# One kernel, five edits: weight words joined in PSUM, shorter scale steps, queries scaled at landing, stores issued by ScalarE, and a list schedule fed with other durations

## The chip, the cores and the metric

The kernel runs on one core of a Trainium2 chip as one program. The time is that of the device for the whole program, in microseconds (us), as the median of a few runs. One execution was also recorded by the hardware profiler; every duration, wait and clock below is from that execution. Engines are named as the profile names them: PE (matmuls), PEld (its weight loads), DVE (VectorE), ACT (ScalarE), POOL (GpSimd) and SP, whose queue issues transfers. A "q" behind a name (SPq, POOLq) is the engine's own instruction queue.

## The reference

Three parts, one behind the other, over 4 batches of 576 tokens with 8 heads of 64. All sums are wanted in float32 accuracy, which the kernel gets by splitting each operand in a high and a low part and multiplying hi·hi, hi·lo and lo·hi.

```
# attention, per batch and head: keep only scores within tau of the row's maximum
scores = (q @ k.T) / 8
scores = where(scores >= max(scores) - tau, scores, -1e9)
x = softmax(scores) @ v                          # 2304 x 512 after all heads

# dense block; w_in 512x2048 and w_out 2048x512 are float64
h = x @ w_in
x = (h * tanh(softplus(h))) @ w_out

# routed block: 8 experts, one per token, and a token with x @ w_skip <= 0 passes through
e = argmax(x @ w_gate); g = softmax(x @ w_gate)[e]
out = x + g * (relu(x @ w1[e]) @ w2[e])
```

## The kernel before

**Units.** Attention runs in 144 units, a unit being 128 query rows against all 576 keys of one head (of two heads for the last, half-filled query tile of a batch). A unit goes score (PE, into the PSUM tile `s`, of which there are two), `u_max` (DVE, row maximum, negated, `nm`), `u_thr` (DVE, two small instructions: the mask's limit and the exponent's bias), `u_exp` (ACT), `u_mask` (DVE, compares with the limit and multiplies), `u_hi` and `u_lo` (a float16 high and low part `hl`), `u_tr` (a transposing DMA on SP's queue, `hl` to `pt`), `u_pv` (PE, times the values). The first 16 units do their mask on PE instead. Queries land raw; the factor 1/8 is applied inside `u_exp`.

**Weights.** `w_in` and `w_out` come as 64-bit floats, 16 chunks each. `w_conv` makes 32-bit words of a chunk with three DVE instructions in SBUF and one addition on POOL (`w_add`); `w_square` then multiplies the words on PE into `gram`, a reduction over partitions on POOL (`all_reduce`) and `w_scale` (`pow2_scale`: seven tiny DVE instructions in a row) give a power of two, and `w_hi`, `w_lo` split the scaled words. The same kind of reduction and scale is taken for each batch of values (`v_scale`), for the gate's weights and for the experts' first weights.

**Dense and routed blocks.** The dense block works on blocks of 128 or 256 tokens as they come out of attention (`m_g1`, `m_exp` to `m_lo`, `m_g2`, `m_out`, `m_store`). `m_store` puts two transfers of a finished tile on SP's queue. Experts follow when attention and the dense block are through.

**What sets the order.** Class `Plan` is a list scheduler that runs while the program is built. Each step is an `op` with an engine (or two engines with a duration each, of which the planner picks one), a duration in ns, a priority, what it comes after, and which ring of buffers it takes and frees. `solve` walks a clock forward and gives each free engine the ready step of best priority; `emit` writes the program in the order found. On the chip every engine runs its steps strictly in that order and waits where a step's input is not there. The reductions over partitions stand in the plan with 400 ns.

Of the kernel before, what the change touches and what calls it, by code (L numbers as in the profile page):

```python
# [20 lines left out]

def pow2_scale(nc, pool, total, s, inv, top=205):
# [168 lines left out]
class Route:  # L191
# [33 lines left out]
    def weights(s):  # L225
        nc = s.nc
        sq = s.wg16[:, 0]
        nc.scalar.activation(out=sq, in_=s.wg, func=AF.Square, accum_out=s.wsc[:, 0:1])
# [16 lines left out]
    def rsq(s, ts, xs):  # L245
        s.begin(ts, xs)
        d = s.st[ts]
        h = d["h"] = s.wk.tile([128, 2, 2, DM], F16, tag="u", bufs=s.nu, name="rh")
        for i, x in enumerate(xs):
            s.nc.scalar.activation(out=h[:, i, 0], in_=x, func=AF.Square, accum_out=d["ss"][:, i])  # L250
# [20 lines left out]
    def psq(s, ts):  # L271
        d = s.st[ts]
        h = d["h"] = s.wk.tile([128, 2, 2, DM], F16, tag="u", bufs=s.nu, name="rh")
        s.nc.scalar.activation(out=h[:, 0, 0], in_=d["x"][0], func=AF.Square, accum_out=d["ss"][:, 0])
# [6 lines left out]
    def rinv(s, ts):  # L281

        d = s.st[ts]
        pow2_scale(s.nc, None, d["ss"], d["inv"], d["rin"], 195)
# [109 lines left out]
class Second:  # L394
# [27 lines left out]
    def stat(s, e, k):  # L422
        t = s.raw.pop(("s", e, k))
        s.nc.scalar.activation(out=t, in_=t, func=AF.Square, accum_out=s.sq[:, e, k:k + 1])  # L424
# [307 lines left out]
def body(ctx, tc, q, k, v, tau, w_in, w_out, w_skip, w_gate, w1, w2, out):  # L732
# [110 lines left out]
    def w_conv(which, c):  # L843

        t = stage[which, c]
        d = wst(c).bitcast(I32)
        lo, hi = t[:, :, 0], t[:, :, 1]
        nc.vector.tensor_scalar(out=d, in0=hi, scalar1=3, scalar2=0x3FFFFFFF, op0=ALU.logical_shift_left,
                                op1=ALU.bitwise_and)
        m = conv_mode(which, c)  # L850
        if m != "D":
            nc.vector.tensor_scalar(out=lo, in0=lo, scalar1=29, scalar2=None, op0=ALU.logical_shift_right)
        if m == "P":
            nc.vector.tensor_scalar(out=hi, in0=hi, scalar1=-(1 << 30), scalar2=None, op0=ALU.bitwise_and)
        else:
            nc.vector.scalar_tensor_tensor(out=d, in0=hi, scalar=-(1 << 30), in1=d, op0=ALU.bitwise_and,
                                           op1=ALU.bitwise_or)
        if m == "D":
            nc.vector.scalar_tensor_tensor(out=d, in0=lo, scalar=29, in1=d, op0=ALU.logical_shift_right,
                                           op1=ALU.bitwise_or)  # L860

    def w_add(which, c):
        t = stage[which, c]
        d = wst(c).bitcast(I32)
        nc.gpsimd.tensor_tensor(out=d, in0=d, in1=t[:, :, 0], op=ALU.add)
        if conv_mode(which, c) == "P":
            nc.gpsimd.tensor_tensor(out=d, in0=d, in1=t[:, :, 1], op=ALU.add)
# [10 lines left out]
    def w_total(which):  # L878
        nc.vector.scalar_tensor_tensor(out=junk32, in0=gram.pop(which)[:, 0:128], scalar=1.0, in1=ident, op0=ALU.mult,
# [59 lines left out]
    def v_square(b, j):  # L939
# [3 lines left out]
        nc.scalar.activation(out=junk, in_=t, func=AF.Square, accum_out=sqv[:, b, j:j + 1])  # L943
# [18 lines left out]
    def q_load(b, qt, c):  # L962
# [7 lines left out]
        stage["q", b, qt, c] = t  # L970

# [39 lines left out]
    def u_max(i):  # L1011
        nm = att.tile([128, 1], F32, tag="nm", bufs=4, name="nm")
# [3 lines left out]
    def u_thr(i):  # L1016

        th = att.tile([128, 2], F32, tag="th", bufs=4, name="th")
        nm, lim = nmx.pop(i), lambda: nc.vector.tensor_scalar(out=th[:, 1:2], in0=nm, scalar1=-1.0, scalar2=ntau[:, 0:1],
                                                              op0=ALU.mult, op1=ALU.add)  # L1020
        if on_pe(i):
            lim()
        nc.vector.tensor_scalar(out=th[:, 0:1], in0=nm, scalar1=0.125, scalar2=None, op0=ALU.mult)  # L1023
        if not on_pe(i):
            lim()
        thr[i] = th
# [684 lines left out]
```

## Time and profile before

| | |
|---|---|
| median of 3 runs | 1104.58 us (1104.17 to 1106.23) |
| profiled execution | 1109.86 us, of which its instructions span 1107.9 us |
| PE / DVE / ACT / POOL busy | 832.0 / 823.4 / 603.7 / 536.2 us |
| mean granted clock of PE | 0.879 of full speed |

The median of the runs is 5.3 us under the profiled execution. The page gives busy time for each engine; "idle before" of a group of instructions is the time its engine stood still just before them, with what released it.

### The profile page before, as it was taken

What the parts mean: (1) busy time and instruction counts of PE and PEld (TensorE: products, weight loads), DVE (VectorE), ACT (ScalarE), POOL (GpSimd) and SP (SyncE); (2) the same over time, 40 slices, a digit from 0 to 9 for tenths busy, and PEclk for the clock granted to TensorE, in tenths of its full rate; (3) what the DMA queues carried; (4) which work ended last, traced back from release to release, by engine and by line L of the source; (5) the groups of instructions that cost most, each with busy time, mean ns of one, the idle gap of its engine ahead of it and who ended that gap; (6) DMA issues with size and microseconds to landing.
All of it is one profiled execution on the core that took longest, in us unless ns stands there. A gap on an engine that the chain in (4) does not pass through costs nothing. (4 is left out here: it accounts for less than half of the span.)

```text
span 1107.9 us, 20418 instructions
## 1 busy us (share of the span) xinstructions
PE 832.0 (75%) x7412; PEld 623.0 (56%) x7412; DVE 823.4 (74%) x1744; ACT 603.7 (54%) x951; POOL 536.2 (48%) x455
## 2 busy tenths in 40 slices
PE   5684375688267888887698989688859988687865
PEld 3353364566155666664476666566626647576764
DVE  5898298898467888878788999898637668474552
ACT  4337144667474676686477677666645743232330
POOL 2561766575435544444645564363325425453443
PEclk9996685689698998899899999889979988888898
DMA  9763295557274495694465674576533418776650
GB/s 260 252 178 93 82 206 138 130 116 195 46 162 93 84 210 116 158 190 81 112 151 133 158 172 108 115 153 140 130 101 109 134 39 264 216 216 197 223 190 26
DMA packets 254148, 162.76 MB, mean 147 GB/s; under 512 B 205135, under 2 KB 205519, under 8 KB 254032
## 3 DMA queue, kind: packets, MB, share of 16 engines
q1 hardware_dynamic: 251136, 154.45, 55.6%
q0 software_dynamic: 2896, 6.83, 2.0%
q8 instruction: 65, 1.06, 0.4%
q14 instruction: 51, 0.42, 0.1%
HBM read 100.71 MB, written 12.57 MB: 102 GB/s over the span
## 5 line engine op out<-in xcount | busy, mean ns | idle before, releaser
L1170 PE MATMUL hp<-xt,win 128*128 128x256 f16 (+1 forms) x1920 | 222.4, 275 | 2.2 <-ACT g L802 2.2
L1227 PE MATMUL o<-wout,g 128*128 128x512 f16 x816 | 199.5, 398 | 18.9 <-POOL g L1216 15.3
L1170 PEld LDWEIGHTS <-win 128*128 128x128 f16 x1920 | 177.3, 103 | 29.4 <-issue 2.8
L1009 PE MATMUL s<-kt,qh 128*128 128x288 f32 x320 | 116.9, 379 | 85.4 <-DVE e L1063 53.6
L1227 PEld LDWEIGHTS <-g 128*128 128x128 f16 x816 | 80.3, 102 | 110.9 <-issue 19.0
L1013 DVE TENSOR_REDUCE nm<-s 128x1 f32<-128x576 f32 x144 | 105.8, 749 | 37.3 <-PE s L1009 36.8
L1096 PE MATMUL xps<-vt,pt 128*128 128x64 f16 (+1 forms) x2016 | 98.0, 209 | 44.0 <-DMA pt<-hl 38.2
L1075 POOL TENSOR_TENSOR hl<-e,hl 128x512 f16<-128x512 f32 x107 | 130.2, 1217 | 0.0
L1074 POOL TENSOR_TENSOR hl<-e,hl 128x64 f16<-128x64 f32 x107 | 47.9, 448 | 166.5 <-ACT hl L802 74.3
L1009 PEld LDWEIGHTS s<-kt,qh 128*128 128x128 f32 x320 | 70.1, 219 | 103.5 <-issue 68.1
L1048 ACT ACTIVATE e<-s,th 128x576 f32<-128x576 f32 x128 | 90.8, 735 | 68.2 <-DVE th L1023 45.3
L1063 DVE SCALAR_TENSOR_TENSOR e<-s,th,e 128x576 f32<-128x576 f32 x128 | 101.4, 810 | 23.4 <-ACT e L1048 23.2
L1096 PEld LDWEIGHTS <-pt 128*128 128x128 f16 x2016 | 85.1, 107 | 58.6 <-DMA pt<-hl 44.9
L1009 PE MATMUL s<-kt,ql 128*128 128x288 f32 x320 | 101.2, 329 | 0.3 <-DVE ql L981 0.3
L802 ACT ACTIVATE hl<-e 128x576 f16<-128x576 f32 x94 | 63.0, 679 | 44.1 <-DVE e L1063 27.8
L576 PEld LDWEIGHTS <-w1q 128*128 128x128 f16 x1056 | 68.9, 107 | 22.3 <-POOL w1q L488 7.2
L1206 POOL TENSOR_TENSOR u<-u,g 128x1024 f32<-128x1024 f32 x22 | 53.7, 2446 | 50.5 <-ACT u L1202 43.2
L599 PE MATMUL o<-w2q,ht 128*128 128x512 f32 x264 | 65.8, 404 | 12.3 <-POOL w2q L488 4.0
L1009 PEld LDWEIGHTS s<-kt,ql 128*128 128x128 f32 x320 | 71.2, 223 | 1.2 <-DVE ql L981 0.7
L576 PE MATMUL g<-xt,w1q 128*128 128x128 f16 x864 | 59.1, 235 | 16.1 <-POOL w1q L488 6.9
L1216 POOL TENSOR_TENSOR g<-u,g 128x1024 f16<-128x1024 f32 x22 | 51.1, 2326 | 29.0 <-ACT g L802 17.2
L424 ACT ACTIVATE ws<-ws 128x512 f32<-128x512 f32 x64 | 40.0, 625 | 44.8 <-DMA ws<-in_w_dram 43.9
(237 smaller groups left out, 1677.8 us busy)
## 6 DMA issues: line engine op xcount, KB each, us to landing
stage<-in_w_dram SPq DMA_DIRECT2D x32, 1024.0 KB, 7.0
ws<-in_w_dram SPq DMA_DIRECT2D x64, 256.0 KB, 3.2
qst<-in_q_dram SPq DMA_DIRECT2D x38, 256.0 KB, 3.9
vst<-in_v_dram SPq DMA_DIRECT2D x35, 256.0 KB, 4.3
win<-in_moe_w_in_dram SPq DMA_DIRECT2D x16, 512.0 KB, 5.9
w<-in_moe_w_out_dram SPq DMA_DIRECT2D x16, 512.0 KB, 4.6
kst<-in_k_dram SPq DMA_DIRECT2D x24, 288.0 KB, 3.1
x2d<-ob SPq DMA_DIRECT2D x18, 256.0 KB, 2.5
```

Source lines behind the costliest of these rows:

```text
L576: s.nc.tensor.matmul(out=p[:, f], lhsT=w[:, c, a, k, f * 128:(f + 1) * 128], rhs=xt[:, 4 * b + k], start=m == 0, stop=m == 11)
L599: s.nc.tensor.matmul(out=o, lhsT=ht[:, a, k], rhs=w[b][:, k // 4, k % 4, :], start=m == 0, stop=m == 23)
L802: nc.scalar.activation(out=out, in_=in_, func=AF.Copy, scale=scale)
L1009: nc.tensor.matmul(out=o, lhsT=x, rhs=y, start=start and n == 0, stop=n == len(ops) - 1)
L1013: nc.vector.tensor_reduce(out=nm, in_=sp[i][:, :, 0:HS], axis=AX.XY, op=ALU.max, negate=True)
L1048: nc.scalar.activation(out=e, in_=sp[i][:, :, 0:HS], func=AF.Exp, scale=0.125, bias=thr[i][:, 0:1])
L1063: nc.vector.scalar_tensor_tensor(out=ep[i], in0=sp.pop(i)[:, :, 0:HS], scalar=thr.pop(i)[:, 1:2], in1=ep[i], op0=ALU.is_ge, op1=ALU.mult, ...
L1075: ENG[eng].tensor_tensor(out=t[:, S + 64:2 * S], in0=e[:, 0:512], in1=t[:, 0:512], op=ALU.subtract)
L1096: nc.tensor.matmul(out=o, lhsT=p[:, blk, :], rhs=vv[:, a, h0:h0 + w], start=(n == 0), stop=(n == len(seq) - 1))
L1170: nc.tensor.matmul(out=hp[j, p][:, i * TB:(i + 1) * TB], lhsT=win[wa][:, kk, f * 128:(f + 1) * 128], rhs=xt[j][:, xa, kk, 0:TB], start=(n ...
L1206: ENG[eng].tensor_tensor(out=u, in0=u, in1=gt[j, r], op=ALU.mult)
L1227: nc.tensor.matmul(out=o, lhsT=g[:, ga, i * TB + s * 128:i * TB + (s + 1) * 128], rhs=wout[f // 8][:, f % 8, wa, :], start=(f == 0 and n = ...
```

## The change

Five edits in one. (1) `w_conv` writes its two intermediate steps to a PSUM tile `wbits` (from the ring `h`, two buffers, that also takes the dense block's `hp`), and its third DVE instruction brings in the low word; POOL's 32 additions are gone. (2) `pow2_scale` has four instructions in place of seven: the sums it gets are taken doubled, by a factor of the square root of two inside the squaring; the routing's `rinv` now calls it once for each tile of a pair. (3) `q_scale`, new, multiplies each landed query tile by 1/8 in place (38 times on ACT, one of the two first tiles on ACT and one on DVE); `u_exp` takes the negated maximum itself as its bias, so `u_thr` is one instruction and `u_exp` comes after `u_max` alone. (4) `m_store` issues its two transfers from ACT. In the same vein `x_evac` adds its 1e-9 on ACT. (5) Most durations given to the planner are others; with them the planner moves steps between engines and changes their order.

```diff
 def pow2_scale(nc, pool, total, s, inv, top=205):
-    nc.vector.tensor_scalar(out=s, in0=total, scalar1=1e-30, scalar2=1e30, op0=ALU.max, op1=ALU.min)
-    nc.vector.tensor_scalar(out=b, in0=b, scalar1=23, scalar2=None, op0=ALU.logical_shift_right)
-    nc.vector.tensor_scalar(out=b, in0=b, scalar1=1, scalar2=None, op0=ALU.add)
-    nc.vector.tensor_scalar(out=b, in0=b, scalar1=1, scalar2=None, op0=ALU.logical_shift_right)
-    nc.vector.tensor_scalar(out=b, in0=b, scalar1=-1, scalar2=top, op0=ALU.mult, op1=ALU.add)
-    nc.vector.tensor_scalar(out=b, in0=b, scalar1=23, scalar2=None, op0=ALU.logical_shift_left)
+    nc.vector.tensor_scalar(out=s, in0=total, scalar1=2e-30, scalar2=2e30, op0=ALU.max, op1=ALU.min)
+    nc.vector.tensor_scalar(out=b, in0=b, scalar1=24, scalar2=23, op0=ALU.logical_shift_right, op1=ALU.logical_shift_left)
+    nc.vector.tensor_scalar(out=b, in0=b, scalar1=-1, scalar2=top << 23, op0=ALU.mult, op1=ALU.add)
     nc.vector.tensor_scalar(out=inv.bitcast(I32), in0=b, scalar1=-1, scalar2=254 << 23, op0=ALU.mult, op1=ALU.add)
...
 def w_conv(which, c):
-        nc.vector.tensor_scalar(out=d, in0=hi, scalar1=3, scalar2=0x3FFFFFFF, op0=ALU.logical_shift_left, op1=ALU.bitwise_and)
-        nc.vector.tensor_scalar(out=lo, in0=lo, scalar1=29, scalar2=None, op0=ALU.logical_shift_right)
-        nc.vector.scalar_tensor_tensor(out=d, in0=hi, scalar=-(1 << 30), in1=d, op0=ALU.bitwise_and, op1=ALU.bitwise_or)
-    def w_add(which, c):
-        nc.gpsimd.tensor_tensor(out=d, in0=d, in1=t[:, :, 0], op=ALU.add)
+        p = ps.tile([128, 512], I32, tag="h", bufs=2, name="wbits")
+        nc.vector.tensor_scalar(out=p, in0=hi, scalar1=3, scalar2=0x3FFFFFFF, op0=ALU.logical_shift_left, op1=ALU.bitwise_and)
+        nc.vector.scalar_tensor_tensor(out=p, in0=hi, scalar=-(1 << 30), in1=p, op0=ALU.bitwise_and, op1=ALU.bitwise_or)
+        nc.vector.scalar_tensor_tensor(out=d, in0=lo, scalar=29, in1=p, op0=ALU.logical_shift_right, op1=ALU.bitwise_or)
...
+    def q_scale(b, qt, c, eng):
+        t = qraw[qt, c][0:64] if first_rows(b, qt) else stage["q", b, qt, c]
+        copy(eng, t, t, 0.125)
...
-        nc.scalar.activation(out=e, in_=sp[i][:, :, 0:HS], func=AF.Exp, scale=0.125, bias=thr[i][:, 0:1])
+        nc.scalar.activation(out=e, in_=sp[i][:, :, 0:HS], func=AF.Exp, bias=nmx[i])
...
-        nc.sync.dma_start(out=R.x2d[r0:r0 + 128, :], in_=t)
-        nc.sync.dma_start(out=out[r0:r0 + 128, :], in_=t)
+        nc.scalar.dma_start(out=R.x2d[r0:r0 + 128, :], in_=t)
+        nc.scalar.dma_start(out=out[r0:r0 + 128, :], in_=t)
...
-        P.op(("lo", i), {"POOL": (1382, 0), "DVE": (737, BD)}, 0, lambda e, i=i: u_lo(i, e), t + 1.13, [("hi", i)], free=[("e", i)])
-        P.op(("tr", i), "SP", 60, lambda i=i: u_tr(i), t + 1.14, [("lo", i)], alloc=[("pt", i)], free=[("hl", i)],
+        P.op(("lo", i), {"POOL": (1740, 0), "DVE": (1820, BD)}, 0, lambda e, i=i: u_lo(i, e), t + 1.13, [("hi", i)], free=[("e", i)])
+        P.op(("tr", i), "SP", 1270, lambda i=i: u_tr(i), t + 1.14, [("lo", i)], alloc=[("pt", i)], free=[("hl", i)],
```

Counted over the whole program, `u_lo` stands 37 times on DVE and 107 on POOL before, 16 and 128 now; `m_g` (u times g) 12 and 22 before, 5 and 29 now. DVE has 264 instructions fewer (1902 and 1638), ACT 111 more (1033 and 1144, transfers counted). The order of PE over scores, values and both dense products is much the same from unit 16 on.

The first place is POOL around the first reductions over partitions (`sc` is the column of scales, `ISA` a library call or the loading of one, `hl` a unit's low part, `win` the low part of `w_in`, `wout<-wout` the `w_add`). Before:

```order
L1074 TENSOR_TENSOR hl<-e,hl 128x64
L1075 TENSOR_TENSOR hl<-e,hl 128x512
L818 ISA
L818 ISA sc<-sc 128x1
L981 ISA
L981 TENSOR_TENSOR ql<-qst,qh 128x512
L900 TENSOR_TENSOR win<-wout,win 128x512 x9
L1074 TENSOR_TENSOR hl<-e,hl 128x64
L1075 TENSOR_TENSOR hl<-e,hl 128x512
L865 TENSOR_TENSOR wout<-wout,w_272 128x512
L865 TENSOR_TENSOR wout<-wout,w_355 128x512
```

Of the change, the same stretch (the reduction for the first weights, behind unit 3's low part):

```order
L1053 TENSOR_TENSOR hl<-e,hl 128x64
L1054 TENSOR_TENSOR hl<-e,hl 128x512
L914 TENSOR_TENSOR kt<-kraw,kt 64x576
L820 ISA
L820 ISA sc<-sc 128x1
L882 ISA
L882 TENSOR_TENSOR win<-wout,win 128x512 x9
L1053 TENSOR_TENSOR hl<-e,hl 128x64
L1054 TENSOR_TENSOR hl<-e,hl 128x512
```

The nine low parts of `w_in` still stand in one run behind a reduction, but now ahead of unit 4 rather than unit 11, and no `w_add` stands behind them; the reduction for batch 1's values comes later, behind unit 8's low part.

The second place is DVE in the middle of attention, at unit 77 (`th` the mask's limit and the bias, `ql` a query tile's low part, `e` the exponentials, `u` and `g` the dense block's activations). Before:

```order
L1013 TENSOR_REDUCE nm<-s 128x1
L806 TENSOR_SCALAR g<-hp 128x512
L1023 TENSOR_SCALAR th<-nm 128x1
L1019 TENSOR_SCALAR th<-nm,ntau 128x1
L981 TENSOR_TENSOR ql<-qst,qh 128x512
L1195 TENSOR_SCALAR u<-u 128x1024
L1013 TENSOR_REDUCE nm<-s 128x1
L1063 SCALAR_TENSOR_TENSOR e,sums<-s,th,e 128x576
```

Of the change, from the same unit's maximum on:

```order
L1000 TENSOR_REDUCE nm<-s 128x1
L806 CAST qh<-qst 128x512
L1006 TENSOR_SCALAR th<-nm,ntau 128x1
L968 TENSOR_TENSOR ql<-qst,qh 128x512
L1042 SCALAR_TENSOR_TENSOR e,sums<-s,th,e 128x576
L1000 TENSOR_REDUCE nm<-s 128x1
L1195 TENSOR_TENSOR g<-u,g 128x1024
```

One small instruction of the unit is gone, the one that gave `u_exp` its bias, and the unit's mask stands ahead of the next unit's maximum instead of behind it.

The third place is ACT where a dense tile is finished (`ob`), of the change; before, the two transfers stood on SP's queue between transposes.

```order
L804 ACTIVATE qst<-qst 128x512
L925 ACTIVATE junk,sqv<-vst 128x512
L804 ACTIVATE qh<-qst 128x512
L1211 ACTIVATE ob<-o,sc 128x512
L1027 ACTIVATE e<-s,nm 128x576
L1219 DMA x2d<-ob 128x512
L1220 DMA out_dram<-ob 128x512
L1027 ACTIVATE e<-s,nm 128x576
```

ACT now holds a query's scaling (first row) and both stores between the exponentials.

## Rows read from the trace of the kernel before

**Rows 1.** Windows: length; PE, PEld, DVE, ACT, POOL busy (instructions); PEclk, DMA share, GB/s.

```profile
0.00:150.00 150.00, 88.06 (x590) 59.33 (x590) 106.29 (x219) 60.20 (x118) 73.78 (x69) 0.85 0.63 174
150.00:350.00 200.00, 127.30 (x1157) 100.29 (x1158) 156.03 (x357) 117.92 (x188) 112.55 (x104) 0.76 0.57 134
350.00:800.00 450.00, 380.87 (x3558) 280.79 (x3557) 381.72 (x867) 307.71 (x487) 223.95 (x208) 0.93 0.62 139
800.00:870.00 70.00, 55.28 (x437) 36.92 (x435) 38.64 (x73) 40.73 (x57) 24.28 (x13) 0.90 0.40 121
870.00:1108.00 238.00, 180.47 (x1679) 145.70 (x1675) 140.73 (x230) 77.11 (x104) 101.66 (x61) 0.89 0.53 164
```

**Rows 2.** PE's waits, 0 to 150: engine, line, releaser: us, times, longest.

```profile
PE gram L876 <- POOL wout L865: 28.4, 5, 19.3
PE s L1009 <- ACT e L1044: 14.3, 6, 12.0
```

**Rows 3.** POOL's timeline, 104 to 130: start, us, instruction [idle before <- releaser].

```profile
106.05 1.39 POOL L818 PARTITION_ALL_REDUCE sc<-sc  x1 [5.86 <-DVE xt L1151]
114.99 1.25 POOL L981 TENSOR_TENSOR ql<-qst,qh 128x512 fp32r<-128x512 f32 x1 [7.55 <-issue]
116.22 10.02 POOL L900 TENSOR_TENSOR win<-wout,win 128x512 f16<-128x512 f32 x9
```

**Rows 4.** PE's waits, 150 to 350, as in group 2.

```profile
PE s L1009 <- DVE e L1063: 27.4, 8, 15.2
PE s L1009 <- DVE th L1023: 13.9, 6, 4.9
```

**Rows 5.** PE's longest wait, 350 to 800.

```profile
PE s L1009 <- DVE e L1063: 26.2, 12, 3.4
```

**Rows 6.** PE's longest wait, 800 to 870.

```profile
PE o L1227 <- POOL g L1216: 13.4, 1, 13.4
```

**Rows 7.** Conversion on DVE by form: busy us, mean ns | idle before, releasers.

```profile
L848 DVE TENSOR_SCALAR wout<-w 128x512 int32<-128x512 int32 x16 | 9.6, 597 | 0.0
L852 DVE TENSOR_SCALAR w<-w 128x512 int32<-128x512 int32 x16 | 12.4, 773 | 0.0
L856 DVE SCALAR_TENSOR_TENSOR wout<-w,wout 128x512 int32<-128x512 int32 x16 | 14.4, 898 | 0.0
```

**Rows 8.** Two lines' durations: ns min/median/max, first and last start in us.

```profile
L848 DVE TENSOR_SCALAR wout<-w x16: 408/448/1133, 105.8 to 181.6; 128x512 int32<-128x512 int32 x16
L806 DVE TENSOR_SCALAR g<-hp x37: 674/684/693, 246.6 to 856.8; 128x512 f32<-128x512 f32 x37
```

**Rows 9.** What leaves an engine, by form, as in group 7.

```profile
L1075 POOL TENSOR_TENSOR hl<-e,hl 128x512 f16<-128x512 f32 x107 | 130.2, 1217 | 0.0
L1074 POOL TENSOR_TENSOR hl<-e,hl 128x64 f16<-128x64 f32 x107 | 47.9, 448 | 166.5 <-ACT hl L802 74.3 <-issue 39.3 <-DVE hl L804 29.9
L1206 POOL TENSOR_TENSOR u<-u,g 128x1024 f32<-128x1024 f32 x22 | 53.7, 2446 | 50.5 <-ACT u L1202 43.2 <-issue 7.4
L1075 DVE TENSOR_TENSOR hl<-e,hl 128x512 f16<-128x512 f32 x37 | 36.9, 998 | 0.0
L865 POOL TENSOR_TENSOR wout<-wout,w 128x512 int32<-128x512 int32 x16 | 23.3, 1461 | 9.0 <-DVE wout L856 8.4 <-DVE th L1023 0.6
L1074 DVE TENSOR_TENSOR hl<-e,hl 128x64 f16<-128x64 f32 x37 | 22.1, 596 | 0.3
L1023 DVE TENSOR_SCALAR th<-nm 128x1 f32<-128x1 f32 x144 | 20.8, 144 | 0.7
L1206 DVE TENSOR_TENSOR u<-u,g 128x1024 f32<-128x1024 f32 x12 | 18.7, 1560 | 0.1
```

**Rows 10.** Nearest rows for what ACT takes on, by form.

```profile
L424 ACT ACTIVATE ws<-ws 128x512 f32<-128x512 f32 x64 | 40.0, 625 | 44.8 <-DMA ws<-in_w_dram 43.9 <-issue 0.9
```

**Rows 11.** One of the two stores' issue on SP's queue, as in group 8.

```profile
L1241 SPq DMA_DIRECT2D out_dram<-ob x18: 422/425/446, 306.6 to 914.0; - x18
```

**Rows 12.** SP's queue, waits, whole span, as in group 2.

```profile
SPq L1240 <- ACT ob L1232: 89.1, 14, 19.5
```

More of the change, by code (lines that the diff above doesn't have):

```diff
@@ L227, in weights @@
         sq = s.wg16[:, 0]
-        nc.scalar.activation(out=sq, in_=s.wg, func=AF.Square, accum_out=s.wsc[:, 0:1])
+        nc.scalar.activation(out=sq, in_=s.wg, func=AF.Square, scale=ROOT2, accum_out=s.wsc[:, 0:1])
         nc.gpsimd.partition_all_reduce(s.wsc[:, 0:1], s.wsc[:, 0:1], 128, bass_isa.ReduceOp.add)
@@ L249, in rsq @@
         for i, x in enumerate(xs):
-            s.nc.scalar.activation(out=h[:, i, 0], in_=x, func=AF.Square, accum_out=d["ss"][:, i])
+            s.nc.scalar.activation(out=h[:, i, 0], in_=x, func=AF.Square, scale=ROOT2, accum_out=d["ss"][:, i])
     def ptr(s, ts, xs, p):
@@ L283, in rinv @@
         d = s.st[ts]
-        pow2_scale(s.nc, None, d["ss"], d["inv"], d["rin"], 195)
+        for i in range(len(ts)):
+            pow2_scale(s.nc, None, d["ss"][:, i], d["inv"][:, i], d["rin"][:, i], 195)
     def rhi(s, ts, i):
@@ L423, in stat @@
         t = s.raw.pop(("s", e, k))
-        s.nc.scalar.activation(out=t, in_=t, func=AF.Square, accum_out=s.sq[:, e, k:k + 1])
+        s.nc.scalar.activation(out=t, in_=t, func=AF.Square, scale=ROOT2, accum_out=s.sq[:, e, k:k + 1])
     def total(s):
@@ L942, in v_square @@
             stage["v", 2, b, j] = t
-        nc.scalar.activation(out=junk, in_=t, func=AF.Square, accum_out=sqv[:, b, j:j + 1])
+        nc.scalar.activation(out=junk, in_=t, func=AF.Square, scale=ROOT2, accum_out=sqv[:, b, j:j + 1])
     def v_scale(b):
@@ L1016, in u_thr @@
     def u_thr(i):
[L1018 to L1026, printed above, removed]
+        thr[i] = att.tile([128, 1], F32, tag="th", bufs=4, name="th")
+        nc.vector.tensor_scalar(out=thr[i], in0=nmx[i], scalar1=-1.0, scalar2=ntau[:, 0:1], op0=ALU.mult, op1=ALU.add)
     def on_pe(i):
@@ L1101, in x_evac @@
         n = 8 if qt < 4 else 4
-        nc.vector.tensor_scalar(out=s[:, 0:n], in0=s[:, 0:n], scalar1=1e-9, scalar2=None, op0=ALU.add)
+        nc.scalar.activation(out=s[:, 0:n], in_=s[:, 0:n], func=AF.Copy, bias=1e-9)
         r = att.tile([128, 8, 1], F32, tag="r", bufs=2, name="r")
@@ L1274, in body @@
                          alloc=[(("qh", "ql")[qt % 2], ("q",) + key)])
+                    P.op(("q_scale",) + key, {"ACT": (650, 0), "DVE": (600, BD)}, 0, lambda e, key=key: q_scale(*key, e), t - 2.6, [("q_load",) + key])
                     continue
@@ L1321, in body @@
                  bulk=4000)
-            P.op(("w_conv",) + key, "DVE", {"P": 1005, "M": 1271, "D": 1800}[conv_mode(which, c)], lambda key=key: w_conv(*key), t,
-                 [("w_load",) + key] + ([("w_lo", 0, c)] if which else []), free=[raw])
             last = ("w_conv",) + key
-            if conv_mode(which, c) != "D":
-                P.op(("w_add",) + key, "POOL", 2550 if conv_mode(which, c) == "P" else 1275, lambda key=key: w_add(*key), t, [last], free=[raw])
-                last = ("w_add",) + key
+            P.op(last, "DVE", 2200, lambda key=key: w_conv(*key), t, [("w_load",) + key] + ([("w_lo", 0, c)] if which else []),
+                 alloc=[("h", ("w",) + key)], free=[raw, ("h", ("w",) + key)])
             P.op(("w_sq",) + key, "PE", 240, lambda key=key: w_square(*key), t, [last] + ([("w_sq", which, c - 1)] if c else []),
```

136 lines of the change are left out of this document (59 added, 77 removed).

## The prediction

> **What bounds the kernel now.** I read the table of stretches first [rows 1], because the share of busy time over the whole run mixes five stages. In the first (0 to 150 us; weights converted, the first 16 units) nobody is near full: PE 88, DVE 106, POOL 74 of 150. In the second (150 to 350) DVE is busiest with 156 of 200 and PE, at a granted clock of 0.76, has 127. In the third (350 to 800, attention and dense block side by side) PE and DVE are level, 381 and 382 of 450, and PE stands still for 69. The fourth (800 to 870) drains the dense block, the fifth (870 to 1108) is the experts, where PE has 180 of 238. So the first three stretches, 800 of 1108 us, are a pipeline in which PE and DVE hold each other up.
>
> Next, who releases PE when it stands still. In the first stretch PE waits 28.4 us for POOL's `w_add` before the Gram products, 19.3 of them at once, and 14.3 for ACT's exponentials, 12.0 at once [rows 2]. What is behind the 19.3 stands in POOL's timeline [rows 3]: a reduction over partitions, 5.86 us idle before it and 7.55 behind it though POOL had work in its queue, then one query part, nine low parts of `w_in` (10.02 us), and only then the rest. In the second stretch PE waits 27.4 us for DVE's mask and 13.9 for its threshold [rows 4]; the longest single one is 15.2. In the third it waits 26.2 us for the mask in 12 pieces [rows 5], in the fourth 13.4 for one low part from POOL [rows 6]. Wherever PE waits long in the middle of the run, the last to come is DVE.
>
> **The change, part by part.**
>
> *What DVE loses.* `u_lo` leaves it 21 times, at 998 + 596 ns: 33.5 us. The second instruction of `u_thr` goes 144 times, at 144 ns: 20.8. `m_g` leaves 7 times, at 1560 ns: 10.9 [rows 9].
>
> *Joining the words in PSUM.* A chunk's three DVE instructions take 597 + 773 + 898 = 2268 ns now [rows 7]. These are means of a spread: the first runs from 408 ns to 1133, while a PSUM operand's instruction of the same size, `g<-hp`, has 674 to 693 [rows 8]. Three of the latter are 2052 ns, so 32 chunks give 6.9 us back. The other end: if every old instruction could run at its fastest (taken as 408, 408 and 684), a chunk is 1500 ns and the new form costs 32 x 552 = 17.7 us more. I take the gain of 6.9, because the old rows are the ones that stand beside the same POOL work. The Trainium skill, "VectorE: DVE Perf Modes", section "Why PSUM operands drop a tier", speaks against this edit: an instruction with a PSUM operand in float32 is held to one element a cycle, where one on SBUF alone can do two. The trace agrees on the flat 684 against the fastest 408. By the rule alone DVE is 17.7 us worse off; by the rows, 6.9 better.
>
> Together DVE loses 33.5 + 20.8 + 10.9 + 6.9 = 72 us (47.5 at the other end). It is busy 106 + 156 + 382 = 644 us before 800, and I spread the relief in that proportion: 12, 17 and 43 us over the three stretches.
>
> *POOL.* It loses 32 `w_add` at some 1461 ns (16 of them in the row), 46.8 us, and gains 21 x (1217 + 448) = 35.0 and 7 x 2446 = 17.1 [rows 9]: 5 us more in all, but earlier in the run less and later more. In the third stretch it has 224 of 450, so that is hidden there.
>
> *ACT.* `q_scale` is 38 instructions of the size of `ws<-ws`, 625 ns [rows 10]: 23.8 us. The 36 stores cost SP at most 0.43 us of its queue each [rows 11]; no row shows a transfer issued from ACT, so I bound it by nothing and by twice that, and take 0.43: 15 us. Together 39 us on an engine that is busy 60 + 118 + 308 = 486 of 800 [rows 1]; hidden behind PE's and DVE's work unless it makes the exponentials late (a rival below). What is queued behind a store on ACT is the next exponential, which PE's score ring waits for.
>
> *SP.* It stood 89.1 us in front of stores whose tile was not yet there [rows 12], with transposes behind them; these blocks go. I count nothing for that: a transpose mostly waits for its low part anyway, and I can't separate the two. A gain from it would be in the deeper case.
>
> *Scale steps and threshold.* Three tiny instructions fewer at each of a few reductions, and the exponential no longer behind `u_thr`. I add nothing beyond the 144 ns above.
>
> *The order.* First stretch: two idle blocks of PE, 12.0 + 19.3 = 31.3 us, become one, since the order rows show the first weights' reduction ahead of unit 4 with the nine low parts behind it and no `w_add`. Its length is worked out from [rows 3]: 5.86 + 7.55 for the reduction's two gaps, 10.02 for the nine, 1.67 for the unit's own low part, 25 us until that unit can go to its transpose. Saved: 6. The reduction for batch 1, which was in the old block, now stops POOL alone for another 13.4 us behind unit 8; that may eat the 6, so this term goes from -20 to +10. Second stretch: the relief of 17 us is smaller than PE's waits for DVE (41.3), of which the single 15.2 us one will hardly move; I take 16. Third: the relief of 43 is larger than the wait it can remove, 26.2; I take nine tenths, 24. Fourth: the 13.4 us wait is for one POOL step in a drain whose steps are the same; the order there differs by a place or two; I take 4. Fifth: PE's order is the same but for some neighbours; 0, with 5 either way.
>
> Sum: 6 + 16 + 24 + 4 = 50 us. From the profiled execution's 1109.9 that is 1059.9; the median of the runs stood 5.3 below it, which gives 1055.
>
> **The rivals.**
>
> *Deeper: a schedule that fits the engines takes all of PE's waits on DVE.* For it: they are what the middle stretches lose, 41.3 and 26.2, and the 13.4 of the drain; PE's clock of 0.76 in the second stretch would come up if PE stood still less. Against: reductions over partitions still stand in the plan at 400 ns and take 13 us more. 6 + 41.3 + 26.2 + 13.4 = 87: 1018.
>
> *The joined words cost what the flat row says against the fastest one.* DVE's relief is 24.6 us smaller, all of it in the first 180 us [rows 8]; then the 16 us of the second stretch are gone: 1071. For it: the flat 684. Against: the means.
>
> *The order buys nothing.* Waits move from DVE to the transposed low parts, of which POOL now makes 128 of 144, and the first stretch's block grows by 8 us instead of shrinking. For it: POOL already waits 74.3 us for ACT's high part and 39.3 for nothing that is shown [rows 9]. Half of the relief in the second and third stretch remains, 8 + 12, less 8: 1109.9 - 12 - 5.3 = 1093.
>
> *Slower: ACT's queue becomes what releases PE.* Place: the third stretch, where an exponential stands behind a query's scaling that waits for its transfer, or behind stores. Price: 39 us of work, and for each of 38 scalings the wait that the 64 instructions of the same kind have for theirs, 43.9 / 64 = 0.69 us [rows 10]: 26 us, so 65. If half of that is on PE's path, 33 us are lost, and the 24 of the third stretch don't come: 1109.9 - 26 + 33 - 5.3 = 1112. It decides from two fifths of the 65 on the path. For it: ACT's share there would be about 75%. Against: 142 of 450 us idle.
>
> **How the numbers follow.** A measurement of this kernel tells about 0.2% (2 us) from no change. Chances: forecast 0.40, its own range 1040 to 1068; deeper 0.18; words dearer 0.10; order buys nothing 0.18; slower 0.09; and 0.05 for terms that cancel to within 0.2%. Faster is 0.40 + 0.18 + 0.10 + 0.18 = 0.86, same 0.05, slower 0.09. For 8 in 10 the range goes from beyond the deeper case (1018 less 15, the open end of the first stretch's term) to beyond the order's (1093 and some): 1003 to 1100.
>
> **What would show each step.** DVE's busy time falls from 823 to about 750 and ACT's rises to about 640, POOL's stays within 15 us of 536. Each of the three conversion lines stands near 684 ns with hardly a spread. The Gram products wait for DVE, not POOL. In the stretch that does units 30 to 140, PE's wait for the mask is a few us and PE's share is over 90%. The stores' lines stand on ACT's queue, at about 0.43 us. I am wrong in the first stretch if PE has an idle block over 35 us near the first weights' scale; in the second and third if PE's idle time there has only changed its releaser, to ACT's exponentials (the slower case) or to the transposed parts (order buys nothing).

## The result and the profile after

The changed kernel takes 1071.27 us (median of 4 runs, 1065.08 to 1072.76); the kernel before, on the same chip, 1104.38. The ratio is 0.9687, 95% interval 0.9647 to 0.9727: 33 us less. The profiled execution took 1071.08 us, 38.8 less than the profiled one of before, whose 1109.9 lay 5.3 above its median; I had taken that offset along, and here there is none. The time lies in the wide range of 1003 to 1100 and just outside the forecast's own 1040 to 1068.

The page's engine line (busy, share of the span, instructions), and the same five stretches as in [rows 1]; the last one is 39 us shorter, since the span now ends at 1069:

```profile
span 1069.1 us, 20207 instructions
PE 826.1 (77%) x7412; PEld 618.9 (58%) x7412; DVE 768.3 (72%) x1480; ACT 634.1 (59%) x1026; POOL 542.6 (51%) x479
```

```profile
0.00:150.00 150.00, 93.94 (x683) 62.87 (x684) 107.12 (x199) 69.19 (x134) 53.56 (x61) 0.97 0.70 196
150.00:350.00 200.00, 139.26 (x1287) 108.49 (x1285) 148.36 (x307) 139.96 (x235) 115.58 (x119) 0.80 0.61 137
350.00:800.00 450.00, 389.51 (x3587) 285.64 (x3586) 349.00 (x738) 333.44 (x539) 260.43 (x234) 0.93 0.64 143
800.00:870.00 70.00, 58.70 (x460) 35.59 (x457) 47.67 (x94) 38.00 (x53) 27.16 (x17) 0.95 0.34 110
870.00:1069.00 199.00, 144.71 (x1403) 126.34 (x1403) 116.18 (x149) 53.50 (x69) 85.89 (x49) 0.84 0.56 170
```

A stretch of the clock holds more work now than before, so what was gained is read by units instead. I cut both traces where `u_max` of a unit starts, at the first expert product and at the end. From before to after unit 16 starts 146.1 to 141.9, unit 48 316.0 to 291.3, unit 143 780.8 to 748.6, the experts 922.9 to 880.6, and the end moves 1107.9 to 1069.1. So 4.2 us were gained up to unit 16, 20.5 from there to unit 48, 7.5 in the 95 units that follow, 10.1 in the drain, and 3.5 were lost in the experts.

These lengths alone mislead, because the same units don't have the same dense work beside them. Of the 864 second dense products (`o<-wout`), 72 lie in units 32 to 48 before and 48 after, 528 and 564 in units 48 to 143, 264 and 252 in the drain. So I also read PE's idle time, a stretch's length less PE's busy time. Units 32 to 48, units 48 to 143 and the drain, first before, then after (columns as in [rows 1], cut at whole us):

```profile
221.00:316.00 95.00, 63.44 (x521) 46.72 (x519) 70.92 (x149) 61.87 (x101) 48.70 (x43) 0.80 0.52 130
316.00:781.00 465.00, 385.29 (x3611) 284.77 (x3610) 395.14 (x916) 311.08 (x490) 237.36 (x221) 0.93 0.62 136
781.00:923.00 142.00, 114.34 (x931) 75.23 (x927) 87.35 (x214) 77.78 (x118) 47.71 (x32) 0.92 0.39 113
...
210.00:291.00 81.00, 57.13 (x495) 44.64 (x495) 69.08 (x120) 64.23 (x112) 53.30 (x48) 0.83 0.64 149
291.00:749.00 458.00, 394.06 (x3699) 290.36 (x3699) 359.71 (x764) 344.93 (x564) 278.26 (x254) 0.92 0.65 142
749.00:881.00 132.00, 110.13 (x873) 73.63 (x872) 83.44 (x197) 73.15 (x103) 47.00 (x34) 0.92 0.39 117
```

PE's idle time falls from 31.6 to 23.9, from 79.7 to 63.9 and from 27.7 to 21.9 us in them. Ahead of them it falls from 58.6 to 56.1 (to unit 16) and from 31.0 to 26.4 (to unit 32); in the experts it rises from 47.3 to 51.0. That is 33 of the 38.8 us; the other 6 are PE's busy time, 832.0 before and 826.1 after.

What answers to [rows 7] and [rows 8], the three lines that join words (one of the two weights; ns minimum/median/maximum):

```profile
L847 DVE TENSOR_SCALAR wbits<-win x16: 680/686/695, 5.5 to 62.5; 128x512 int32<-128x512 int32 x16
L848 DVE SCALAR_TENSOR_TENSOR wbits<-win,wbits x16: 695/696/697, 6.2 to 63.3; 128x512 int32<-128x512 int32 x16
L849 DVE SCALAR_TENSOR_TENSOR wout<-win,wbits x16: 686/686/690, 6.9 to 64.0; 128x512 int32<-128x512 int32 x16
```

They are flat, 2.07 us a chunk. What answers to [rows 2], [rows 4] and [rows 5], PE's waits up to unit 16, in units 16 to 48 and in units 48 to 143 (us, times, longest):

```profile
PE gram L858 <- DVE wout L849: 24.4, 11, 7.7
PE xps L1075 <- DMA pt<-hl: 19.4, 4, 8.6
PE s L996 <- ACT e L1024: 8.8, 4, 7.1
...
PE xps L1075 <- DMA pt<-hl: 22.9, 11, 9.0
PE s L996 <- DVE e L1042: 13.3, 5, 7.5
...
PE xps L1075 <- DMA pt<-hl: 16.7, 10, 2.2
PE s L996 <- DVE e L1042: 12.1, 7, 7.3
PE xps L1075 <- DVE th L1006: 8.7, 4, 4.7
```

The Gram products no longer wait for POOL, and no wait is longer than 9 us, where before there were single ones of 19.3, 15.2 and 13.4. In units 48 to 143 the waits for the mask and for transposed parts fell by 17.6 and 7.7 us; before, they were:

```profile
PE s L1009 <- DVE e L1063: 29.7, 13, 3.5
PE xps L1096 <- DMA pt<-hl: 24.4, 16, 4.1
```

VectorE's waits for TensorE's scores rose there from 9.1 us in 12 pieces to

```profile
DVE nm L1000 <- PE s L996: 37.8, 44, 3.7
```

### The profile page after: what moved, and what is told of

It reads as the page before. It is cut to its first block, busy times and chain, and to the rows that moved or that the text cites. A ratio compares the mean times of both kernels' runs of the same rounds, so it can differ in the third digit from the quotient of the medians.

```text
span 1069.1 us, 20207 instructions
## 1 busy us (share of the span) xinstructions
PE 826.1 (77%) x7412; PEld 618.9 (58%) x7412; DVE 768.3 (72%) x1480; ACT 634.1 (59%) x1026; POOL 542.6 (51%) x479
## 5 line engine op out<-in xcount | busy, mean ns | idle before, releaser
L1149 PE MATMUL hp<-xt,win 128*128 128x256 f16 (+1 forms) x1920 | 218.6, 271 | 3.0 <-DVE g L808 2.9
L1149 PEld LDWEIGHTS <-win 128*128 128x128 f16 x1920 | 173.5, 101 | 28.6 <-DVE g L808 3.1
L1054 POOL TENSOR_TENSOR hl<-e,hl 128x512 f16<-128x512 f32 x128 | 157.1, 1227 | 0.0
L1075 PE MATMUL xps<-vt,pt 128*128 128x64 f16 (+1 forms) x2016 | 97.5, 208 | 74.4 <-DMA pt<-hl 61.3
L996 PE MATMUL s<-kt,qh 128*128 128x288 f32 x320 | 113.7, 369 | 35.3 <-DVE e L1042 25.5
L1053 POOL TENSOR_TENSOR hl<-e,hl 128x64 f16<-128x64 f32 x128 | 52.6, 411 | 159.3 <-DVE hl L806 55.6
L1027 ACT ACTIVATE e<-s,nm 128x576 f32<-128x576 f32 x128 | 92.8, 735 | 30.3 <-DVE nm L1000 28.4
L996 PE MATMUL s<-kt,ql 128*128 128x288 f32 x320 | 97.5, 319 | 2.7 <-POOL ql L968 2.6
L804 ACT ACTIVATE hl<-e 128x576 f16<-128x576 f32 x99 | 67.0, 678 | 39.4 <-DVE e L1042 18.7
L1185 POOL TENSOR_TENSOR u<-u,g 128x1024 f32<-128x1024 f32 x29 | 70.0, 2427 | 22.5 <-ACT u L1181 22.4
L601 PEld LDWEIGHTS o<-w2q,ht 128*128 128x128 f32 x264 | 51.9, 201 | 27.8 <-issue 9.5
```

The source lines that it names most:

```text
L601: s.nc.tensor.matmul(out=o, lhsT=ht[:, a, k], rhs=w[b][:, k // 4, k % 4, :], start=m == 0, stop=m == 23)
L804: nc.scalar.activation(out=out, in_=in_, func=AF.Copy, scale=scale)
L996: nc.tensor.matmul(out=o, lhsT=x, rhs=y, start=start and n == 0, stop=n == len(ops) - 1)
L1054: ENG[eng].tensor_tensor(out=t[:, S + 64:2 * S], in0=e[:, 0:512], in1=t[:, 0:512], op=ALU.subtract)
L1075: nc.tensor.matmul(out=o, lhsT=p[:, blk, :], rhs=vv[:, a, h0:h0 + w], start=(n == 0), stop=(n == len(seq) - 1))
L1149: nc.tensor.matmul(out=hp[j, p][:, i * TB:(i + 1) * TB], lhsT=win[wa][:, kk, f * 128:(f + 1) * 128], rhs=xt[j][:, xa, kk, 0:TB], start=(n ...
```

## The experiments

Five readings stood to be told apart. **A**: the order made from realistic durations carries the gain. **B**: the work taken off VectorE carries it. **C**: either alone only moves the waits, both are needed. Later, **D**: what the order needs from the edits is edit 1, POOL free of joining words; **E**: it needs the small edits 2 to 4. To part the order from the edits without a new draw of the plan, some kernels don't plan but replay the list of the other kernel's plan (3185 operations with their engines in the changed kernel), by replacing one line.

The table gives each run's median, the ratio to the kernel before with its interval, and the lengths in the profiled execution: to unit 32, to 48, to 143, to the experts, to the end. Those are worked out from one execution each, and 21 executions of the kernel before on one chip took 1102.0 to 1114.2 us, so a difference of a few us in one stretch is not to be relied on.

| run | us | ratio | to 32 | to 48 | to 143 | drain | experts |
|---|---|---|---|---|---|---|---|
| before | 1104.4 | 1 | 221.3 | 94.7 | 464.8 | 142.1 | 185.0 |
| e1 edits, old order | 1099.8 | 0.9924 [0.9889, 0.9960] | 212.1 | 97.4 | 460.3 | 146.2 | 182.5 |
| e2 new order, old instructions | 1099.8 | 0.9936 [0.9912, 0.9961] | 241.2 | 82.4 | 460.9 | 126.3 | 187.9 |
| e3 durations only | 1109.2 | 1.0021 [0.9989, 1.0052] | 229.9 | 93.6 | 466.6 | 132.1 | 180.6 |
| e5 change without edit 1 | 1097.3 | 0.9937 [0.9906, 0.9967] | 241.0 | 82.5 | 457.9 | 130.6 | 187.2 |
| e6 new order + edit 1 alone | 1071.0 | 0.9719 [0.9667, 0.9770] | 211.6 | 81.7 | 462.3 | 127.8 | 184.7 |
| **after** | 1071.3 | 0.9687 [0.9647, 0.9727] | 209.7 | 81.6 | 457.4 | 131.9 | 188.6 |
| e4 after, stores on SP | 1063.5 | 0.9622 [0.9573, 0.9671] | 212.1 | 81.8 | 453.2 | 128.2 | 186.5 |
| e7 after, no clamp | 1064.0 | 0.9644 [0.9585, 0.9704] | 209.1 | 82.0 | 456.5 | 130.7 | 184.1 |
| e9 after, old engines | 1083.8 | 0.9792 [0.9737, 0.9847] | 209.0 | 80.7 | 473.1 | 131.4 | 191.3 |
| e10 before, no clamp | 1100.1 | 0.9956 [0.9928, 0.9984] | 219.7 | 90.2 | 462.5 | 139.7 | 186.5 |
| e11 e4 replanned | 1081.5 | 0.9778 [0.9731, 0.9826] | 209.0 | 73.2 | 479.7 | 128.3 | 188.5 |
| e12 sums costed | 1058.8 | 0.9587 [0.9548, 0.9627] | 195.5 | 83.6 | 470.1 | 118.6 | 185.7 |
| e8 sums on PE | 1051.8 | 0.9544 [0.9495, 0.9593] | 185.1 | 81.9 | 483.3 | 115.8 | 182.6 |

**Order and edits apart (e1, e2, e3).** e1 is the changed kernel with the list of before, e2 the kernel before with the list of the changed one, e3 the kernel before planned anew with the new durations.

```diff
-    P.solve()
+    follow(P, ORDER)
```

> All edits of the instructions (words joined in PSUM, short scale, query scaling at landing, one-instruction thresholds, stores and the x_evac addition on ScalarE), issued in the order and on the engines that the kernel before's plan chose; only q_scale is put in ahead of its q_hi and w_add falls away. Theory A (the order made from realistic durations carries the gain): at most a third of the 33 us, so 1093 to 1104 us. Theory B (the VectorE work that the edits take off carries it): 1072 to 1083 us. Theory C (either alone moves VectorE's waits only elsewhere, both are needed): 1095 or more here and in the run of the new order too.

> The kernel before's instructions, none edited, issued in the order and on the engines that the changed kernel's plan chose (w_add right behind its w_conv, the two threshold instructions right behind the row maximum, stores on SP). Theory A: 1075 to 1088 us. Theory B: 1094 to 1106 us. Theory C: 1095 or more.

> The kernel before's instructions, planned anew with the changed kernel's durations (and 2350, 1480, 380 and 760 ns for w_conv, w_add, thr and mst, which the changed kernel has in another form). It is what edit 5 alone would have given. Theory A: 1075 to 1088 us, within 6 us of the run with the borrowed order. Theory B: 1094 to 1106 us. If it differs from the borrowed order by more than 8 us, the plan's luck is as large as the effects.

Each half alone gives under 1%, and the new durations alone nothing. That is C. The new durations missed both of their windows, and their plan lies 9.4 us over the borrowed order, beyond the 8 that I had set as the sign of the plan's luck. By stretch, the edits in the old order gain 9.2 us ahead of unit 32 and 0.2 behind it. The order with the old instructions loses 19.9 ahead of unit 32 and gains 29.1 behind it. e2's waits of PE up to unit 32 (its first 241 us) show the loss:

```profile
PE gram L876 <- POOL wout L865: 41.4, 14, 8.3
PE xps L1096 <- DMA pt<-hl: 39.3, 12, 8.7
```

**Which edit the order needs (e5, e6).** e5 is the changed kernel, in its order, with words joined on POOL; e6 is the kernel before, in the new order, with words joined in PSUM and nothing else. The edit, as e5 takes it back:

```diff
-        nc.vector.scalar_tensor_tensor(out=d, in0=lo, scalar=29, in1=p, op0=ALU.logical_shift_right, op1=ALU.bitwise_or)
+            nc.vector.tensor_scalar(out=lo, in0=lo, scalar1=29, scalar2=None, op0=ALU.logical_shift_right)
...
+    def w_add(which, c):
...
+        nc.gpsimd.tensor_tensor(out=d, in0=d, in1=t[:, :, 0], op=ALU.add)
```

> The changed kernel in its own order, with edit 1 alone undone: the words of the weights are again joined by a POOL addition behind two VectorE instructions and a shift, each w_add right behind its w_conv. Theory D (the interaction is edit 1: the new order fills POOL with low parts, which only works once POOL no longer joins words, because TensorE's Gram products wait for POOL): it gives back 18 to 28 us, nearly all of it before unit 32, so 1089 to 1099 us, with PE waiting some 40 us for POOL's wout. Theory E (the small VectorE edits 2 to 4 make the order pay): 1071 to 1080 us.

> The kernel before's instructions in the changed kernel's order, with edit 1 alone applied (words joined in PSUM by VectorE, no POOL addition); two-instruction thresholds, six-step scales, unscaled queries, stores on SP. Theory D: 1068 to 1080 us, the changed kernel within 1%; edits 2 to 4 together then are worth what is left, at most 8 us. Theory E: 1088 to 1100 us.

D, by both. Without edit 1 the change is back at 1097. All of the 30.0 us by which the profiled runs differ lies ahead of unit 32 (31.3 there), with PE again behind POOL:

```profile
PE xps L1095 <- DMA pt<-hl: 41.1, 13, 9.2
PE gram L878 <- POOL wout L867: 40.3, 15, 8.2
```

With edit 1 alone the new order gives the changed kernel's time; edits 2 to 4 together are worth nothing that can be measured (0.9719 and 0.9687, their intervals overlap widely). That may be a gain and a loss: e6 has its stores on SP, and e4 below, which differs from it by edits 2 and 3 and the addition in `x_evac`, stands at 0.9622.

**Stores (e4).** In the changed kernel's order, with one word changed in each of two lines:

```diff
-        nc.scalar.dma_start(out=out[r0:r0 + 128, :], in_=t)
+        nc.sync.dma_start(out=out[r0:r0 + 128, :], in_=t)
```

> The changed kernel with its 36 output stores issued by SP again, everything else in the same order. My prediction counted 89.1 us of SP's waits in front of the stores as nothing and ScalarE's 36 issues as 15 us of ScalarE work off the path: then the time is the changed kernel's within 0.3% (1068 to 1075 us). Rival: a store that waits on SP for its block holds the transposing DMAs behind it, and PE's waits for pt (61.3 us) grow: 1078 to 1090 us.

Its median, 1063.5, lies 7.8 us below the changed kernel's and below each run of it, outside both windows; the two intervals overlap by 0.0024, and the two were not run side by side, so a gain is likely, and its size is not shown. That SP's waits in front of stores cost more than the issues on ACT, the rival here, is ruled out; that they cost nothing is not shown. On ACT's queue the two stores' issues are as I sized them, 36 x 0.39 = 14 us:

```profile
L1219 ACTq DMA_DIRECT2D x2d<-ob x18: 332/333/350, 304.7 to 869.5; - x18
...
L1220 ACTq DMA_DIRECT2D out_dram<-ob x18: 444/451/1423, 305.1 to 869.9; - x18
```

Unit 143 starts at 748.6 in the changed kernel and at 747.1 here; 5.8 of the 7.3 us that the profiled runs differ by come behind it, in the drain and the experts.

**What VectorE's time is worth (e7, e10).** The 36 instructions that bound the exponentials are left out, once in the changed kernel, once in the kernel before, each in its order.

```diff
     def m_min(j, r):
-        u = gu[j, r]
-        nc.vector.tensor_scalar(out=u, in0=u, scalar1=CU, scalar2=None, op0=ALU.min)
+        return
```

> The changed kernel without the 36 VectorE instructions that bound the exponentials from above (that part of the computation is left out), all else in its order. It takes some 42 us of VectorE's work away, most of it in the stretch of units 48 to 143 and the drain. If VectorE still sets the pace there, as my third term has it (nine tenths of what it is relieved of): 1040 to 1055 us. If TensorE and the transposes set it since the change: 1064 to 1072 us.

> The kernel before, in its own order, without the 36 VectorE instructions that bound the exponentials from above (that part is left out). If VectorE set its pace in units 30 to 140, as my prediction's third term assumed, taking some 40 us from VectorE gives 25 to 36 us: 1068 to 1080 us. If VectorE only carries out what the order makes late, it gives under 8 us: 1097 to 1104 us (the same removal gave 7 us in the changed kernel).

VectorE's busy time falls by 25.0 us in the kernel before (823.4 to 798.4) and by 34.2 in the changed one:

```profile
PE 824.3 (78%) x7412; PEld 615.8 (58%) x7412; DVE 734.1 (69%) x1444; ACT 634.0 (60%) x1026; POOL 537.3 (51%) x479
```

The times fall by 5 us in the kernel before and by 7 in the changed one, where the intervals, 0.9644 and 0.9687, overlap widely. In units 48 to 143 VectorE has 15.7 and 23.0 us less to do, and they get shorter by 2.3 and 0.9. So this work did not set the pace in either kernel, although in the kernel before VectorE ended 45 of TensorE's 79 us of waits there.

**Sequence or engines (e9).** The changed kernel, its list replayed with the engine column of before: `follow` as in e1, with 305 engines exchanged.

> The changed kernel's instructions in its own order, but each operation that may run on one of several engines is put back on the engine that the kernel before's plan chose (305 of them change place, among them the 47 splits that move between POOL and VectorE). If the sequence in which units, blocks and stages follow one another carries the order's 29 us behind unit 32: 1070 to 1085 us. If the division of the work between VectorE, POOL and ScalarE carries it: 1090 to 1105 us. An assignment that no plan balanced can also be worse than either: above 1105 us would leave it open.

Up to unit 48 nothing changes: those gains are the sequence's. The drain keeps its length, but with less PE work in it; by idle time (25.2 us, before 27.7) it keeps under half of its gain. 15.7 us are lost in units 48 to 143, 10.1 of them PE's idle time, where the old division of work suits the new sequence less. A part of that may be that no plan balanced this mixture; the run can't say.

**Sums over partitions and the plan's luck (e8, e11, e12).** All three are e4 planned anew. e8 makes six sums by a TensorE product with ones, e11 changes one harmless number, e12 also tells the plan what a sum costs. A cut of each, in this order:

```diff
-        nc.gpsimd.partition_all_reduce(dst, dst, 128, bass_isa.ReduceOp.add)
+        p = ps.tile([128, 512], F32, tag="h", bufs=2, name="allr")
+        nc.tensor.matmul(out=p[:, 0:1], lhsT=ones32, rhs=col(n), start=True, stop=True)
...
-        P.op(("w_scale", which), "DVE", 1500, lambda which=which: w_scale(which), t, [("w_all", which)])
+        P.op(("w_scale", which), "DVE", 700, lambda which=which: w_scale(which), t, [("w_all", which)])
...
-        P.op(("v_all", b), "POOL", 400, lambda b=b: all_reduce(col(SQ + 1 + b)), ts, [("v_tot", b)])
+        P.op(("v_all", b), "POOL", 13800, lambda b=b: all_reduce(col(SQ + 1 + b)), ts, [("v_tot", b)], lat=-7000.0)
```

> The changed kernel with stores on SP (as in the fourth run), and six of the sums over partitions (four of the values, two of the weights) made by a TensorE product with ones into PSUM, read by a VectorE copy, instead of by POOL's library function; planned anew. In the trace of the changed kernel each such sum held POOL for some 13 us of loading, with low parts queued behind. If these blocks of POOL hold up the path: 1040 to 1058 us. If POOL's idle or blocked time is off the path: 1058 to 1068 us; the plan's own luck is some 10 us either way, as the third run showed.

> A control of the plan's luck: the changed kernel with stores on SP, planned anew with one harmless number changed, the duration of the six scale computations on VectorE (700 ns planned in place of 1500); all instructions stay. If the 12 us that the sums on TensorE gained came from the sums: 1058 to 1070 us. If they came from another draw of the plan: 1048 to 1057 us.

> As the control run, but the plan is told what a sum over partitions costs POOL in the trace: 13800 ns of POOL, its result ready after 6800; the sums stay on POOL. If the low parts queued behind a sum that the plan took for 400 ns were what hurt, the plan now puts them elsewhere and gains most of the same 12 us: 1050 to 1058 us. If it is the sum's own 7 us on the path from the weights to their scale: 1058 to 1070 us.

e11's control misses its window on the wrong side: one number that changes no instruction costs 18 us against e4, all of it in units 48 to 143 (PE's idle time there is 78.8 us against 61.8). So a difference of that size between two plans shows nothing about what was changed, and e8's 12 us and e12's 5 us against e4 can't be put down to the sums. e12's median lies 0.8 us over the line between its two windows and decides neither. Against e11, which shares their other numbers, e12 is 22.7 us faster with nothing changed but the plan's cost of a sum. That is again one plan against one other, hardly further apart than e4 and e11. What speaks for the sums is the place: e8 and e12 reach unit 32 earlier than any other kernel here (185.1 and 195.5 against 209.0 or more). e8 is the fastest version found, 4.6% under the kernel before.

## Why the prediction was right in direction, and where its steps failed

**What the order gained behind unit 32.** By PE's idle time e2 gains 7.9 us in units 32 to 48, 13.5 in units 48 to 143 and 9.9 in the drain, and loses 1.4 in the experts. In the first and the third of these stood the two longest waits of before behind unit 16, 15.2 and 13.4, and they are gone. I had read both as VectorE's or POOL's plain lateness. POOL's timeline of before shows one and the same thing in front of each, a sum over partitions (start, us, instruction [idle before]):

```profile
282.27 0.40 POOL L229 PARTITION_ALL_REDUCE wsc<-wsc  x1 [6.65 <-issue]
290.02 2.33 POOL L1206 TENSOR_TENSOR u<-u,g 128x1024 f32<-128x1024 f32 x1 [7.35 <-issue]
...
815.53 0.43 POOL L430 PARTITION_ALL_REDUCE tot<-tot  x1 [7.34 <-issue]
822.84 0.24 POOL L1460 IOTA jrow<- 128x128 f32 x1 [6.88 <-issue]
823.06 2.33 POOL L1206 TENSOR_TENSOR u<-u,g 128x1024 f32<-128x1024 f32 x1
825.36 2.11 POOL L1216 TENSOR_TENSOR g<-u,g 128x1024 f16<-128x1024 f32 x1
```

Behind the first stands `m_g` of a block; ACT stands before that block's high part, with two exponentials queued behind it, and TensorE's scores wait for their masks (ACT's and PE's timeline of before):

```profile
292.39 1.06 ACT L802 ACTIVATE g<-u 128x1024 f16<-128x1024 f32 x1 [13.90 <-POOL u L1206]
293.35 1.36 ACT L1048 ACTIVATE e<-s,th 128x576 f32<-128x576 f32 x2
```

```profile
295.08 0.58 PE L1009 MATMUL s<-kt,qh 128*128 128x288 f32 x1 [15.17 <-DVE e L1063]
...
827.53 4.45 PE L1227 MATMUL o<-wout,g 128*128 128x512 f16 x10 [13.42 <-POOL g L1216]
```

In the changed kernel's order the same sum is followed by a low part, and ACT's high part comes later; its wait for `u` shrinks from 13.90 us to 3.94 (POOL's, then ACT's timeline):

```profile
283.65 0.40 POOL L230 PARTITION_ALL_REDUCE wsc<-wsc  x1 [6.35 <-ACT sums L1081]
291.30 0.30 POOL L1053 TENSOR_TENSOR hl<-e,hl 128x64 f16<-128x64 f32 x1 [7.25 <-ACT junk L925]
```

```profile
295.05 1.06 ACT L804 ACTIVATE g<-u 128x1024 f16<-128x1024 f32 x1 [3.94 <-POOL u L1185]
```

With the edits in the old order both waits are still there (14.2 and 11.9), with the old instructions in the new order they are not. The link to the sums is read from the rows; no run here took these two sums away alone. The new plan still counts a sum at 400 ns, so that less hangs behind them now may be a lucky draw. Nor do the two waits explain the 29.1 us. In units 32 to 48 PE's waits for transposed parts rose from 2.4 to 9.8 us in the changed kernel while the 15.2 went. e3 has neither wait (its longest in these stretches are 6.5 and 5.2), and yet PE's idle time in them is that of before, 30.5 and 29.1 us. And the 13.5 us in units 48 to 143 are taken from waits none of which was longer than 4.1 us before. That the sequence brings the gain is shown; what in it does is open.

**First stretch, 6 predicted, 4.2 to unit 16 (2.6 by idle time).** Half of the mechanism held. Where I expected one block of 25 us, PE stands still for 7.15 and 8.58 us around the nine low parts, and Gram waits for VectorE. But those waits for VectorE are 24.4 us, where POOL's were 28.4, and 19.4 for transposed parts are new, so little of the saving is left. I missed how much depends on `w_add` being gone; with it the same order is 31 us later at unit 32 (e5). PE's timeline at the nine low parts:

```profile
79.33 4.21 PE L996 MATMUL s<-kraw,qraw 64*128 64x288 f32 x8 [7.15 <-ACT e L1024]
92.12 0.93 PE L1075 MATMUL xps<-vt,pt 128*128 128x64 f16 x14 [8.58 <-DMA pt<-hl]
```

**Second stretch, 16 predicted, 20.5 to unit 48 (12.4 by idle time).** The size was near, the reason wrong. I gave it to VectorE's relief and wrote that the 15.2 us wait "will hardly move". It went. In units 32 to 48 the stretch is 13.1 us shorter, 7.7 of them idle time, and the edits in the old order gain nothing there (e1). The 7.4 ahead of them need edit 1: without it units 16 to 32 take 77.0 us (e5), with it 67.8.

**Third stretch, 24 predicted, 7.5 measured (15.8 by idle time): the step that failed.** "Nine tenths" of the mask waits would go, because VectorE was last to come. 17.6 of 29.7 us went, but not by taking work off VectorE alone. With the edits in the old order VectorE has 17.7 us less to do in these units, and without the clamps 15.7 (e10); the waits stay at 27.6 and 28.2. In the new order they are shorter even with the old instructions and with the old engines. In turn e1, e2 and e9:

```profile
PE s L996 <- DVE e L1042: 27.6, 16, 3.6
PE s L1009 <- DVE e L1063: 16.6, 11, 8.0
PE s L996 <- DVE e L1042: 17.3, 9, 10.5
```

So in the old order VectorE came last without its load being the reason, as far as 16 to 18 us less can show. In the new one the division of work counts too: with the old engines PE's idle time there is 10.1 us longer (e9). Of the 15.8 us of idle time half did not come out as a shorter stretch, since 8.3 us more of PE's work fell into it. PE was to be over 90% busy and to wait a few us for the mask; it is at 394 of 458, 86% (before 83%), and still waits 12.1 us for it and 16.7 for transposed parts.

**Fourth, 4 predicted, 10.1 (5.8 by idle time); fifth, 0 predicted, -3.5.** The drain's steps are the same, but what stood behind its sum over partitions is not, and less dense work is left for it. The experts' loss is inside the 5 either way; no run asks for its cause.

**The engines' sums.** VectorE fell by 55 us, not 72. Words, threshold and moved low parts went as sized, but what stays on VectorE got longer: the clamp's mean rose from 959 to 1079 ns, `m_lo`'s from 1332 to 1790. That POOL's work beside them does it is seen for the clamp (last section). Joining in PSUM cost 2.07 us a chunk against 2.05 predicted. ACT at 634 and POOL at 543 are as predicted; `q_scale` took 23.5 us (38 times 622 ns) against 23.8. That stores on ACT lie off the path was probably wrong, by some 7 us if e4's difference holds.

**The rivals.** "Order buys nothing" had a true part: PE's waits for transposed parts rose from 38.2 to 61.3 us over the run, all of it ahead of unit 48. Yet the order bought 29 behind unit 32. The dearer words give 1071, the measured time, but that is chance: a chunk's three instructions average 2.07 us against 2.39 before, over both weights. ACT's queue did not become what releases PE in the third stretch, and the deeper case would have needed the 25.5 us of mask waits that are left.

**The sum.** The terms gave 50 us, and by PE's idle time they measure 2.6, 12.4, 15.8, 5.8 and -3.7, 33 in all. That the total is within a factor of two owes something to luck: the two largest terms had the wrong reason. The 15 us by which I lowered the end of the range is not the open end of the first term, which is +10.

## What to carry to other kernels

The engine that releases a wait is not therefore the engine that sets the pace: take some of its work away in a run before counting its relief as time. Where two orders are compared by stretches, compare an engine's idle time in them and not only their lengths, since work moves across the cuts. Judge a list schedule and an edit by replaying one fixed order under both, since here a plan with one harmless number changed moved the time by 18 us, more than half of what the change gained. Where a plan counts an operation at a thirtieth of what it holds its engine for, look at what stands behind that operation, but measure before counting its waits as time: e3 lost the two long ones and gained nothing there.

## What was not expected of the hardware

Every one of the eight sums over partitions on POOL, before and after, has 5.9 us or more of idle POOL ahead of it and 6.9 or more behind it, not only the first; the instruction itself is shown with some 0.4 us, in one case 1.39 [rows 3].

VectorE's clamp (128x1024, float32, SBUF to SBUF), a single form, has two durations. In the changed kernel the 18 of 36 that ran beside almost no POOL arithmetic (POOL's two-input instructions, under 5% of their time) took 688 ns on average, the 17 that had it beside them for over 30% of theirs 1516; in the kernel before 685 (19) and 1343 (15). The mean hides two cases. Of the 17, the five that started ahead of POOL's instruction took 678 to 683 ns, the twelve that started behind one 778 to 4711. Below, the first clamp started behind a low part's second instruction on POOL and ended 0.55 us after it. The second started just ahead of a low part, whose first instruction then took 0.81 us in place of 0.31:

```profile
310.48 0.31 POOL L1053 TENSOR_TENSOR hl<-e,hl 128x64 f16<-128x64 f32 x1 [0.21 <-ACT hl L804]
310.74 1.16 POOL L1054 TENSOR_TENSOR hl<-e,hl 128x512 f16<-128x512 f32 x1
310.94 1.51 DVE L1174 TENSOR_SCALAR u<-u 128x1024 f32<-128x1024 f32 x1
...
455.81 0.68 DVE L1174 TENSOR_SCALAR u<-u 128x1024 f32<-128x1024 f32 x1
455.85 0.81 POOL L1053 TENSOR_TENSOR hl<-e,hl 128x64 f16<-128x64 f32 x1 [0.40 <-DVE hl L806]
```

The kernel before is less clean: two of the thirteen that started behind POOL's instruction, by 0.04 and 0.26 us, still took 677 and 689 ns. The word joins with a PSUM operand kept to 680 to 697 ns throughout. The Trainium skill, "SBUF — State Buffer", section "SBUF: two separate sides", calls the port pair that the two engines share an exclusive lock: whichever starts first, a GpSimd instruction or a VectorE one that uses two ports, has it for the whole of its instruction. The order of the starts and the two durations agree with it, but for those two.
